# One product for read-out and state update in a chunked RWKV-7 kernel, with a new order of its early turns

## The chip, the cores and the metric

The kernel runs on one core of a Trainium2 chip. Its time is the device time of one execution in microseconds; before the change it is 758.51 us, the median of 3 runs (757.66 to 759.96). The profile shown is of an execution with a span of 757.1 us. Engine names: PE is TensorE, PEld its weight loads, DVE is VectorE, ACT is ScalarE, POOL is GpSimd, SP is SyncE, which here only issues DMAs.

## The reference, cut to what matters

Attention with a recurrent state, then a feed-forward block with a softmax gate and a layer norm:

```python
batch, n_heads, seq, head_dim = (4, 8, 768, 40)
for t in range(S):
    y[:, :, t] = einsum('bhd,bhde->bhe', rt, state)              # read-out, from the state before t
    Sa = einsum('bhde,bhe->bhd', state, at)
    state = state * wt[:, :, None, :] - einsum('bhd,bhe->bhde', Sa, bt) + einsum('bhd,bhe->bhde', vt, kt)

# x: y as 3072 rows of 320
h = x @ w_in                                                     # 320 x 1024
e = exp(h - max(h)); sm = e / (sum(e) + 1e-09)
solu = h * sm
ln = (solu - mean(solu)) / sqrt(var(solu) + 1e-06) * g_ln
out = ln @ w_out                                                 # 1024 x 320
```

The two weight matrices come as 64-bit floats; the kernel brings them in as pairs of 32-bit words and narrows them on the chip.

## The kernel before

The 768 steps are cut into 12 chunks of L = 64 steps. Each chunk has two turns ("slots" below), i = 0 to 23, of 16 heads each; P = 128, Q = 32, D = 40, H = 8, G = 4. Within a chunk the recurrence is solved with the inverse of a triangular matrix. What a slot does is written as generators, and a string gives the order in which their steps are put into the engines' queues. Every engine works through its own queue in that order.

The recurrence of slot i, its read-out, and the crossed term that adds the carried state:

```python
def carried(i, crossed):
    d = st[i]
    for m in range(2):
        for p in range(2):
            for z in range(2):
                c, g = z ^ crossed, 2 * m + z
                nc.tensor.matmul(d["y"][half(p), c, g * L:g * L + L], lhsT=d["sT"][half(z), c, m, half(p)], ...)  # L507

def recurrence(i):
    ...                                                # r1: px (L526), then x = x_own + px on VectorE (L528)
    ...                                                # r2: psT, copied to sT by ScalarE (L539)
    ...                                                # r3: pu (L547), copied to nuT by ScalarE
    y = d["y"] = duo("pyo")
    if ci:
        carried(i, True)
    lamu = d["lamu"] = wide("lamu", 1)
    scores("lamu", nuT, d["rT"], lamu)                 # r4: product on PE, masked by VectorE (L281)
    yield
    t = bank("pnu")
    for g in range(G):
        nc.tensor.transpose(out=t[:, g * P:(g + 1) * P], in_=nuT[:, g, :], identity=ident)
    nc.scalar.copy(out=nu.rearrange("p h c -> p (h c)"), in_=t)                       # r5, L565
    yield
    if ci < NCH - 1:
        t = duo("pst")                                                                # r6
        for j, x in enumerate((vb, nu)):
            for g in range(G):
                for p in range(2):
                    for c in range(2):
                        nc.tensor.matmul(t[half(p), c, g * D:g * D + D], lhsT=kb[half(c), j, 2 * g + p, :],
                                         rhs=x[half(c), G * p + g, 0:D], ...)         # L573
        new = t[:, :, 0:G * D].rearrange("q c (g d) -> q c g d", d=D)
        ...                                            # tot = new + sm on VectorE (L579), sm = tot * factor on GpSimd

def readout(i):
    kb, t = d["kb"], d["y"]
    for j, lam in ((1, d["lamu"]), (0, d["lamv"])):
        for g in range(G):
            for p in range(2):
                h = G * p + g
                for c in range(2):
                    nc.tensor.matmul(t[half(p), c, g * L:g * L + L], lhsT=kb[half(c), j, 2 * g + p, :],
                                     rhs=lam[half(c), h % 2, h // 2, :], ...)         # L593
        if j and i >= 2:
            carried(i, False)
    nc.vector.tensor_tensor(out=of_round[n]["x"]..., in0=t..., in1=d["exT"]..., op=ALU.mult)   # L600
```

The read-out and the state update multiply the same stationary matrices kb, the one with lam (64 columns a head), the other with v and nu (40 columns a head).

The inverse of one chunk takes 32 steps: one that prepares u from the gathered blocks, 30 of two VectorE operations each (L413, L415), and one that sends it off. It serves two slots. bring_inverse fetches it back for a slot, in the layout which that slot's solve needs.

```python
def invert(n):
    ...
    u_dram = of_round[n]["u"] = dram.tile(...)
    for p in range(2):
        nc.sync.dma_start(out=u_dram...[:, :, p], in_=u[half(p)])
    ut = two.tile([P, Q, Q // 2], FP32, tag="ut", name="ut", bufs=1)
    nc.vector.tensor_copy(out=ut, in_=u.rearrange("p c t -> p t c"))                  # L421
    nc.sync.dma_start(out=ut_dram, in_=ut)
    yield

def bring_inverse(i, other=nc.sync):
    ...                                                # 4 DMAs tinv <- ut_dram on `other`, 4 DMAs tinvT <- u_dram on SyncE
```

The narrowing of a weight piece has four steps: two VectorE operations (L162, L164); three ScalarE operations (L167 to L169); one VectorE operation (L171); two GpSimd operations. weights() keeps two pieces under way, so that its steps alternate: one with VectorE's operations of both, and one with ScalarE's operations of the new piece and GpSimd's of the old. After the last piece it forms the column means of the scaled weights (mean, L239) and scales the weights on VectorE (L242).

```python
    pg = bank("pg")
    nc.tensor.transpose(out=pg[:, 0:NF], in_=g_rows, identity=ident[0:NF, 0:NF])
    nc.scalar.copy(out=g_col, in_=pg[:, 0:NF])
    gb = two.tile([P, NF, P], FP32, tag="e", name="gb", bufs=1)
    nc.scalar.mul(out=gb, in_=g_col.unsqueeze(2).to_broadcast([P, NF, P]), mul=1.0 / DFF)
    yield
    mean = bank("mean")
    ...                                                # 8 matmuls into mean
```

The order of a slot (r recurrence, y read-out, I inverse, W weights, a attend of the next slot, s its solve, f and g fronts of later slots, h hidden product of slot i - 6, b and o its end, L a load). The list of numbers says how many steps each I stands for:

```python
EARLY = ("r r a r f r W I r y W r I W W a f a s W a f W a W I f I W s f L W a f", ...)       # i < 6
STEADY = "r b r a r f b b o r o I o r o y o r I o h a f L a s a h f a I h f I s h f h a f h" # i >= 6

def inverse_steps(i):
    if i < 3:
        return [[6, 6, 6, 6], [0, 3, 4, 3], [6, 6, 5, 5]][i]
    return [0, 6, 4, 4] if i % 2 else [6, 6, 3, 3]
...
bring_inverse(0, nc.scalar)                            # in the prologue
...
for i in range(N):
    ...
    if i == 1:
        steps(inv, 8)                                  # the rest of the second inverse
    ...
    if i >= LAG:                                       # LAG = 6
        steps(ws, 99)                                  # what is left of weights()
```

The steps of attend are: kT, vT (each a transposition, copied by ScalarE), psi, rT, lamv, and px0; those of a front end with kx (VectorE, L371), bT and nt. PSUM is used in 2 single banks ("bank"), 2 pairs ("duo") and one pair for h.

Of the kernel before, what the change touches and what calls it, by code (L numbers as in the profile page):

```python
# [52 lines left out]
def kernel(  # L53
# [21 lines left out]

    nc = tc.nc
    B, H, S, D = r.shape
    DM = H * D  # L80
# [57 lines left out]
    ti_t = zeroed(nc.vector, "tinvT", [P, 2, G, L], 2)  # L138
    tn_t = [const.tile([P, H, 2, Q // 2], FP32, name=f"tinv{i}") for i in range(2)]
    sm_t = zeroed(nc.vector, "sm", [P, 2, G, 64], 2)  # L140
    nu_t = [const.tile([P, H, 64], FP32, name=f"nu{i}") for i in range(1)]
# [36 lines left out]
    def weights():  # L178
# [52 lines left out]
        pg = bank("pg")  # L231
        nc.tensor.transpose(out=pg[:, 0:NF], in_=g_rows, identity=ident[0:NF, 0:NF])
        nc.scalar.copy(out=g_col, in_=pg[:, 0:NF])
        gb = two.tile([P, NF, P], FP32, tag="e", name="gb", bufs=1)
        nc.scalar.mul(out=gb, in_=g_col.unsqueeze(2).to_broadcast([P, NF, P]), mul=1.0 / DFF)
        yield
# [45 lines left out]
            out=dst, in0=t[:, :, 0:G * L].rearrange("q p (g c) -> q p g c", g=G),  # L282
            in1=tri.unsqueeze(1).unsqueeze(1).to_broadcast([P, 2, G, L]), op=ALU.mult)

    def wide(name, bufs=1):
        return two.tile([P, 2, G, L], FP32, tag=name, name=name, bufs=bufs)

    st = [dict() for _ in range(N)]
    of_round = [dict() for _ in range(NCH)]
# [107 lines left out]
    def invert(n):  # L397

        nb = of_round[n]["nb"]
        u = two.tile([P, Q // 2, Q], FP32, tag="u", name="u", bufs=1)
        nc.vector.tensor_scalar(out=u[half(0)], in0=nb[half(0)].rearrange("b (c z) t -> b c z t", z=2)[:, :, 0],
                                scalar1=-1.0, scalar2=None, op0=ALU.mult)
        nc.vector.memset(u[half(1)], 0.0)
        for p in range(2):
            nc.vector.memset(u[half(p)].rearrange("b c t -> b (c t)")[:, p:Q * Q // 2:Q + 2], 1.0)
        yield
        for j in range(1, Q - 1):
            m, rows = Q - 1 - j, (j + 1) // 2  # L410
            t = two.tile([P, Q * Q // 8], FP32, tag="prod", name="prod", bufs=1)[:, 0:rows * m] \
                .rearrange("p (c r) -> p c r", c=rows)
            nc.vector.tensor_tensor(out=t, in0=nb[:, j:j + 1, j + 1:Q].to_broadcast([P, rows, m]),  # L413
                                    in1=u[:, 0:rows, j:j + 1].to_broadcast([P, rows, m]), op=ALU.mult)
            nc.vector.tensor_tensor(out=u[:, 0:rows, j + 1:Q], in0=u[:, 0:rows, j + 1:Q], in1=t, op=ALU.subtract)  # L415
            yield
        u_dram = of_round[n]["u"] = dram.tile([64, Q, Q], FP32, tag="u_dram", name="u_dram")
        for p in range(2):
            nc.sync.dma_start(out=u_dram.rearrange("b (c z) t -> b c z t", z=2)[:, :, p], in_=u[half(p)])
        ut = two.tile([P, Q, Q // 2], FP32, tag="ut", name="ut", bufs=1)  # L420
        nc.vector.tensor_copy(out=ut, in_=u.rearrange("p c t -> p t c"))  # L421
        ut_dram = of_round[n]["ut"] = dram.tile([P, Q, Q // 2], FP32, tag="ut_dram", name="ut_dram")
        nc.sync.dma_start(out=ut_dram, in_=ut)
        yield

    def bring_inverse(i, other=nc.sync):

        d = st[i]
        tinvT, tinv = d["tinvT"], d["tinv"] = ti_t[i % 2], tn_t[i % 2]
        n, s = divmod(i, 2)  # L430
        ut, u = of_round[n]["ut"], of_round[n]["u"]
        for q in (0, 2):
            for p in range(2):
                other.dma_start(out=tinv[quarter(q), :, p],
                                  in_=ut[half(p)][homes(q, s)].rearrange("h s t -> s h t"))
        for q in range(4):
            nc.sync.dma_start(out=tinvT[quarter(q), :, :, quarter(q % 2)].rearrange("s p g t -> s (p g) t"),
                              in_=u[homes(q, s)].rearrange("h s t -> s h t"))

    def attend(i):  # L440

        d = st[i]
        kT = transposed("kT", d["kb"][:, 0])
        yield
        vT = transposed("vT", given(i, "v"))
        yield
        psi = d["psi"] = wide("psi")
        scores("psi", kT, d["aT"], psi)
        yield
        rT = d["rT"] = transposed("rT", given(i, "r"), "rT", 2)  # L450
        yield
        lamv = d["lamv"] = wide("lamv", 2)
        scores("lamv", vT, rT, lamv)
        yield
        t = duo("px0")
        for g in range(G):
            for p in range(2):
                for c in range(2):
                    nc.tensor.matmul(t[half(c ^ p), p, g * D:g * D + D], lhsT=psi[half(c), p, g, :],
                                     rhs=given(i, "v")[half(c), G * p + g, 0:D], start=True, stop=True)  # L460
# [38 lines left out]
    def carried(i, crossed):  # L499


        d = st[i]
        for m in range(2):
            for p in range(2):
                for z in range(2):
                    c, g = z ^ crossed, 2 * m + z
                    nc.tensor.matmul(d["y"][half(p), c, g * L:g * L + L], lhsT=d["sT"][half(z), c, m, half(p)],  # L507
                                     rhs=d["rT"][half(z), (G * p + g) // 2, half(c)],
                                     start=crossed and m == 0, stop=False, skip_group_check=True)

    def recurrence(i):
        d = st[i]
        ci, s = divmod(i, 2)
        sm, nu = sm_t[s], nu_t[0]
        kb, vb = d["kb"], given(i, "v")
        x0 = x0_t[i % 2]
        if ci < NCH - 1:
            fac = small.tile([P, 2, G], FP32, tag="fac", name="fac")
# [37 lines left out]
        if ci:  # L556
            d["sT"] = sT
            carried(i, True)
        lamu = d["lamu"] = wide("lamu", 1)
        scores("lamu", nuT, d["rT"], lamu)  # L560
        yield
        t = bank("pnu")
        for g in range(G):
            nc.tensor.transpose(out=t[:, g * P:(g + 1) * P], in_=nuT[:, g, :], identity=ident)
        nc.scalar.copy(out=nu.rearrange("p h c -> p (h c)"), in_=t)  # L565
        yield
        if ci < NCH - 1:
            t = duo("pst")
            for j, x in enumerate((vb, nu)):
                for g in range(G):  # L570
                    for p in range(2):
                        for c in range(2):
                            nc.tensor.matmul(t[half(p), c, g * D:g * D + D], lhsT=kb[half(c), j, 2 * g + p, :],  # L573
                                             rhs=x[half(c), G * p + g, 0:D], start=j == 0 and g == 0, stop=j == 1,
                                             skip_group_check=True)
            new = t[:, :, 0:G * D].rearrange("q c (g d) -> q c g d", d=D)
            if ci:
                tot = two.tile([P, 2, G, D], FP32, tag="tot", name="tot", bufs=1)
                nc.vector.tensor_tensor(out=tot, in0=new, in1=sm[:, :, :, 0:D], op=ALU.add)  # L579
# [4 lines left out]

    def readout(i):
        d, (n, s) = st[i], divmod(i, 2)
        kb, t = d["kb"], d["y"]
        for j, lam in ((1, d["lamu"]), (0, d["lamv"])):
            for g in range(G):
                for p in range(2):  # L590
                    h = G * p + g
                    for c in range(2):
                        nc.tensor.matmul(t[half(p), c, g * L:g * L + L], lhsT=kb[half(c), j, 2 * g + p, :],  # L593
                                         rhs=lam[half(c), h % 2, h // 2, :], start=i < 2 and g == 0 and j == 1,
                                         stop=j == 0, skip_group_check=True)
# [4 lines left out]
        nc.vector.tensor_tensor(out=of_round[n]["x"][:, :, s].rearrange("q g (c t) -> q c g t", c=2),  # L600
                                in0=t[:, :, 0:G * L].rearrange("q c (g t) -> q c g t", g=G),
                                in1=d["exT"].rearrange("q g (c t) -> q c g t", c=2), op=ALU.mult)
        yield

# [87 lines left out]
    def fronts(i):  # L692

        return [j for j in ((4, 5) if i == 0 else (i + AHEAD,)) if j < N]

    EARLY = ("r r a r f r W I r y W r I W W a f a s W a f W a W I f I W s f L W a f",
             "r r a r f g r W I r y W r I W W a f g a s W a f g W a W I f g I W s f g L W a f g")
    STEADY = "r b r a r f b b o r o I o r o y o r I o h a f L a s a h f a I h f I s h f h a f h"
    front_of = {}

    front_of = {}
# [14 lines left out]
    def inverse_steps(i):  # L716

        if i < 3:
            return [[6, 6, 6, 6], [0, 3, 4, 3], [6, 6, 5, 5]][i]
        return [0, 6, 4, 4] if i % 2 else [6, 6, 3, 3]  # L720

    def later(n):
        load(n, "b", "k")
# [2 lines left out]
    with tc.manual_schedule():  # L726
# [12 lines left out]
        turns("f g f g f f g g", {}, f=f, g=g)  # L739
        load(2, "w", "a", "b", "k")  # L740
        turns("a a I a a W", dict(I=99), a=at, I=inv, W=ws)
        bring_inverse(0, nc.scalar)
        turns("a f g a f g f g", {}, f=f, g=g, a=at)
        scatter(1)
        gather(1)
# [5 lines left out]
        for i in range(N):  # L751
            m, more, js = i - LAG, i + 1 < N, fronts(i)
            if i % 2 and (i + 3) // 2 < NCH:
                gather((i + 3) // 2)
            if i == 1:
                steps(inv, 8)
            now = hidden(m) if m >= 0 else None
            parts = dict(r=recurrence(i), y=readout(i), I=inv, W=ws, h=now, b=after, o=before)
            if i >= LAG:
# [51 lines left out]
```

## Time and profile before

| | us |
|---|---|
| time, median of 3 | 758.51 |
| span of the profile | 757.1 |
| PE busy | 630.4 (83%) |
| PEld busy | 451.1 (60%) |
| DVE busy | 455.5 (60%) |
| ACT busy | 270.1 (36%) |
| POOL busy | 118.4 (16%) |
| mean granted TensorE clock | 0.886 of full |
| pst (L573), busy, 1408 records | 30.6 |
| read-out (L593), busy, 1536 records | 32.5 |

Busy time is a sum over instructions; a matmul's end is modelled, so its mean time is longer than its share of a packed stream. A 32-bit float matmul leaves two records. A wait is given with the engine or DMA whose event came last before it ended. The share of the whole span mixes an early stage (slots 0 to 5, in which the weights are narrowed too) with the later slots, in which the feed-forward products run beside the recurrence; each has to be read by itself.

### The profile page before, as it was taken

The page shows a single profiled execution, that of the slowest core. Times are in us where ns is not written, and L with a number is a line of the kernel's source. Part 1 is how long each engine was busy: PE and PEld are TensorE (multiplying, and loading weights), DVE is VectorE, ACT ScalarE, POOL GpSimd, SP SyncE. Part 2 cuts the span into 40 slices and gives each one's busy share as a digit, 9 for nine tenths or more (in the row PEclk, how much of TensorE's full clock was granted, in tenths as well). Part 3 has the DMA queues.
Part 4 walks back from the last instruction along what each step waited for, and adds up shares of the span by engine and source line. Part 5 has one row for each costly group of instructions (what it writes and reads, how often), then busy time and mean ns, then how long its engine had stood idle before and what let it go on. Part 6 is the DMA issues. An engine that isn't in the chain of part 4 may idle for free.

```text
span 757.1 us, 28253 instructions
## 1 busy us (share of the span) xinstructions
PE 630.4 (83%) x12281; PEld 451.1 (60%) x12281; DVE 455.5 (60%) x1258; ACT 270.1 (36%) x631; POOL 118.4 (16%) x204
## 2 busy tenths in 40 slices
PE   6335758566584899999999999999999899998997
PEld 4334646455473666666676767767667566654554
DVE  3654764746645485768758677687585772334442
ACT  4113325333353142434333533444343332332222
POOL 4102132321232011111111011101110000000000
PEclk9656575795775799999999999999999999999999
DMA  8946455355354434544553635545414322101001
GB/s 138 162 73 119 88 109 103 66 104 118 68 114 94 65 63 93 93 94 77 110 101 57 127 72 94 101 85 98 92 35 82 69 48 38 27 15 26 11 8 35
DMA packets 269804, 60.01 MB, mean 79 GB/s; under 512 B 255465, under 2 KB 265329, under 8 KB 269681
## 3 DMA queue, kind: packets, MB, share of 16 engines
q1 hardware_dynamic: 264592, 52.66, 38.3%
q10 hardware_dynamic: 5088, 5.55, 2.9%
q8 instruction: 97, 1.59, 0.9%
q14 instruction: 27, 0.21, 0.1%
HBM read 40.08 MB, written 13.37 MB: 71 GB/s over the span
## 4 chain that ended last, share of the span: by engine, by line
PE 65%; DVE 17%; DMA 6%; ACT 5%; issue 4%; SPq 2%; ACTq 0%; POOL 0%; DVEq 0%
PE po L666 14%; PE h L621 14%; DVE prod L413 5%; DVE u L415 5%; PE plnT L661 3%; PE pyo L593 3%; PE pcx L340 3%; PE plamv L279 2%; PE pst L573 2%; PE pcum L327 2%; DMA blk<-blk_dram 2%; PE py L481 2%; DMA blk_dram<-nt 2%; PE pyo L507 2%; PE px L526 1%
## 5 line engine op out<-in xcount | busy, mean ns | idle before, releaser
L621 PE MATMUL h<-w_in,xT 128*128 128x512 f32 (+1 forms) x288 | 126.8, 627 | 3.9 <-DVE e L638 3.9
L666 PE MATMUL po<-w,lnT 128*128 128x320 f32 x384 | 118.8, 442 | 0.0
L415 DVE TENSOR_TENSOR u<-u,prod 128x30 f32<-128x30 f32 (+4 forms) x360 | 98.3, 273 | 12.4
L413 DVE TENSOR_TENSOR prod<-blk,u 128x30 f32<-128x30 f32 (+4 forms) x360 | 99.1, 275 | 10.3
L666 PEld LDWEIGHTS po<-w,lnT 128*128 128x128 f32 x384 | 67.6, 190 | 23.6 <-issue 2.9
L330 POOL TENSOR_TENSOR kx<-raw_b,inv 128x320 f32<-128x320 f32 x24 | 20.9, 873 | 255.2 <-ACT inv L328 204.6
L621 PEld LDWEIGHTS h<-w_in,xT 128*128 128x128 f32 (+1 forms) x288 | 37.8, 189 | 30.6 <-issue 28.7
L631 DVE TENSOR_REDUCE nmax<-h 128x1 f32<-128x1024 f32 x24 | 29.4, 1223 | 40.7 <-PE h L621 40.7
L671 ACT ACTIVATE osb<-po,rs 128x320 f32<-128x320 f32 x24 | 12.6, 527 | 106.0 <-PE po L666 94.6
L481 PE MATMUL py<-tinv,nt 32*32 32x32 f32 x768 | 21.1, 207 | 29.7 <-DMA tinv<-ut_dram 17.8
L281 DVE TENSOR_TENSOR lamv<-plamv,cst 128x512 f32<-128x512 f32 x24 | 16.6, 690 | 43.0 <-PE plamv L279 43.0
L340 PE MATMUL pcx<-cst,lw 128*128 128x132 f32 x192 | 35.2, 318 | 8.2 <-ACT vT L262 8.1
L600 DVE TENSOR_TENSOR x<-pyo,kx 128x512 f32<-128x512 f32 x24 | 16.6, 691 | 42.0 <-PE pyo L593 41.0
L340 PEld LDWEIGHTS pcx<-cst,lw 128*128 128x128 f32 x192 | 30.7, 220 | 17.3 <-ACT vT L262 8.3
L635 ACT ACTIVATE e<-h,nmax 128x1024 f32<-128x1024 f32 x24 | 26.7, 1114 | 37.3 <-DVE nmax L631 37.3
L662 ACT COPY lnT<-plnT 128x512 f32<-128x512 f32 x48 | 27.6, 586 | 33.9 <-PE plnT L661 33.8
L638 DVE TENSOR_TENSOR e<-h,e 128x1024 f32<-128x1024 f32 x24 | 29.4, 1224 | 14.6 <-ACT e L635 14.0
L653 POOL TENSOR_TENSOR rs<-c,mhalf 128x1 f32<-128x1 f32 x24 | 13.2, 548 | 157.0 <-DVE c L652 157.0
L481 PEld LDWEIGHTS py<-tinv,nt 32*32 32x32 f32 x768 | 17.8, 118 | 32.0 <-issue 18.5
L496 ACT ACTIVATE tinvT<-pz 32x256 f32<-32x256 f32 x48 | 17.9, 373 | 51.3 <-PE pz L481 51.0
L661 PE MATMUL plnT<-cst,e 128*128 128x128 f32 x192 | 30.6, 290 | 5.7 <-DVE e L638 5.4
L580 POOL TENSOR_TENSOR sm<-tot,fac 128x320 f32<-128x320 f32 x20 | 14.7, 737 | 118.6 <-DVE tot L579 98.7
(107 smaller groups left out, 1160.9 us busy)
## 6 DMA issues: line engine op xcount, KB each, us to landing
blk<-blk_dram SPq DMA_DIRECT2D x24, 256.0 KB
raw_w<-in_w_dram SPq DMA_DIRECT2D x24, 160.0 KB
raw_a<-in_a_dram SPq DMA_DIRECT2D x24, 160.0 KB
raw_b<-in_b_dram SPq DMA_DIRECT2D x24, 160.0 KB
raw_k<-in_k_dram SPq DMA_DIRECT2D x24, 160.0 KB
v<-in_v_dram SPq DMA_DIRECT2D x24, 160.0 KB
r<-in_r_dram SPq DMA_DIRECT2D x24, 160.0 KB
out_dram<-osb SPq DMA_DIRECT2D x24, 160.0 KB
```

Of the source, the lines that this page charges most:

```text
L340: nc.tensor.matmul(t[:, g * 132:g * 132 + 132], lhsT=pair(lw, 2 * j + g), rhs=cst[:, lo:lo + 132], start=True, stop=True)
L413: nc.vector.tensor_tensor(out=t, in0=nb[:, j:j + 1, j + 1:Q].to_broadcast([P, rows, m]), in1=u[:, 0:rows, j:j + 1].to_broadcast([P, rows, ...
L415: nc.vector.tensor_tensor(out=u[:, 0:rows, j + 1:Q], in0=u[:, 0:rows, j + 1:Q], in1=t, op=ALU.subtract)
L481: nc.tensor.matmul(t[quarter(out), c:c + Q], lhsT=lhs(p, g), rhs=rhs(p, g), start=True, stop=True)
L593: nc.tensor.matmul(t[half(p), c, g * L:g * L + L], lhsT=kb[half(c), j, 2 * g + p, :], rhs=lam[half(c), h % 2, h // 2, :], start=i < 2 and ...
L621: nc.tensor.matmul(h[:, j * 512:j * 512 + 512], lhsT=of_round[i // 2]["xT"][rows, kt, i % 2 * P:i % 2 * P + P], rhs=w_in[rows, 4 if kt == ...
L631: nc.vector.tensor_reduce(out=nmax, in_=h, axis=AX.X, op=ALU.max, negate=True)
L635: nc.scalar.activation(out=e, in_=h, func=AF.Exp, bias=nmax, accum_out=esum)
L638: nc.vector.tensor_tensor(out=q, in0=h, in1=e, op=ALU.mult)
L661: nc.tensor.transpose(out=t[:, j * P:(j + 1) * P], in_=q[:, f * P:(f + 1) * P], identity=ident)
L662: nc.scalar.copy(out=lnT[:, fs.start:fs.stop].rearrange("p f t -> p (f t)"), in_=t)
L666: nc.tensor.matmul(o[:, 0:DM], lhsT=lnT[:, f, :], rhs=w2[:, f, :], start=f == 0, stop=f == NF - 1)
```

## The change

The 40 columns of v and of nu are put behind the 64 columns of lamv and lamu of each head, in one tile of 104 columns. v is copied there by GpSimd, nu by ScalarE straight from PSUM. The read-out then yields both: 64 columns of y and 40 columns of the new state, 104 a head, 416 of the 512 of a PSUM bank. The separate state product pst goes away. In the last chunk only the 64 columns are computed.

Beside it, the order of the queues changes. A slot of the early stage has ten steps of weights() instead of nine, so that ScalarE's part of a piece stands at other places than VectorE's. The second inverse is done within slot 0 (8 steps at each I), and the 8 steps at the head of slot 1 go. In the steady order one of the four I goes and its steps are spread over the other three. ut is copied and sent before the second half of u. SyncE issues all DMAs of the first bring_inverse, not ScalarE. weights() has one step more, between g_col and gb.

```diff
-    def wide(name, bufs=1):
-        return two.tile([P, 2, G, L], FP32, tag=name, name=name, bufs=bufs)
+    def wide(name, width, bufs=1):
+        return two.tile([P, 2, G, width], FP32, tag=name, name=name, bufs=bufs)
@@ invert
-        for p in range(2):
-            nc.sync.dma_start(out=u_dram.rearrange("b (c z) t -> b c z t", z=2)[:, :, p], in_=u[half(p)])
         ut = two.tile([P, Q, Q // 2], FP32, tag="ut", name="ut", bufs=1)
         nc.vector.tensor_copy(out=ut, in_=u.rearrange("p c t -> p t c"))
         ut_dram = of_round[n]["ut"] = dram.tile([P, Q, Q // 2], FP32, tag="ut_dram", name="ut_dram")
-        nc.sync.dma_start(out=ut_dram, in_=ut)
+        for p in range(2):
+            nc.sync.dma_start(out=u_dram.rearrange("b (c z) t -> b c z t", z=2)[:, :, p], in_=u[half(p)])
+            if p == 0:
+                nc.sync.dma_start(out=ut_dram, in_=ut)
@@ weights
         nc.scalar.copy(out=g_col, in_=pg[:, 0:NF])
+        yield
         gb = two.tile([P, NF, P], FP32, tag="e", name="gb", bufs=1)
@@ attend
+        lamv = d["lamv"] = wide("lamv", L + D, 2)
+        nc.gpsimd.tensor_copy(out=lamv[:, :, :, L:], in_=given(i, "v").rearrange("q (m z) d -> q z m d", z=2)[:, :, :, 0:D])
...
-        lamv = d["lamv"] = wide("lamv", 2)
-        scores("lamv", vT, rT, lamv)
+        scores("lamv", vT, rT, lamv[:, :, :, 0:L])
@@ recurrence
-        lamu = d["lamu"] = wide("lamu", 1)
-        scores("lamu", nuT, d["rT"], lamu)
+        lamu = d["lamu"] = wide("lamu", L + D)
+        scores("lamu", nuT, d["rT"], lamu[:, :, :, 0:L])
...
-        nc.scalar.copy(out=nu.rearrange("p h c -> p (h c)"), in_=t)
+        nc.scalar.copy(out=lamu[:, :, :, L:], in_=t.rearrange("q (m z c) -> q z m c", m=G, z=2)[:, :, :, 0:D])
...
-            t = duo("pst")
-            for j, x in enumerate((vb, nu)):
-                ...                                    # the 32 matmuls of L573
-            new = t[:, :, 0:G * D].rearrange("q c (g d) -> q c g d", d=D)
+            new = y[:, :, 0:G * (L + D)].rearrange("q c (g w) -> q c g w", g=G)[:, :, :, L:]
@@ readout
-        kb, t = d["kb"], d["y"]
+        kb, t, W = d["kb"], d["y"], L + D
+        used = W if n < NCH - 1 else L
...
-                        nc.tensor.matmul(t[half(p), c, g * L:g * L + L], lhsT=kb[half(c), j, 2 * g + p, :],
-                                         rhs=lam[half(c), h % 2, h // 2, :], ...)
+                        nc.tensor.matmul(t[half(p), c, g * W:g * W + used], lhsT=kb[half(c), j, 2 * g + p, :],
+                                         rhs=lam[half(c), h % 2, h // 2, 0:used], ...)
@@ order
-    EARLY = ("r r a r f r W I r y W r I W W a f a s W a f W a W I f I W s f L W a f", ...)
-    STEADY = "r b r a r f b b o r o I o r o y o r I o h a f L a s a h f a I h f I s h f h a f h"
+    EARLY = ("r r a r W f r W W I r y W r W I a f a W s a f a W I W f s W I f a W L f", ...)
+    STEADY = "r b r a r f b b o r o I o r o y o r I o h a f L a s a h f a I h f s h f h a f h"
...
-            return [[6, 6, 6, 6], [0, 3, 4, 3], [6, 6, 5, 5]][i]
-        return [0, 6, 4, 4] if i % 2 else [6, 6, 3, 3]
+            return [[8, 8, 8, 8], [0, 3, 4, 3], [6, 6, 5, 5]][i]
+        if i < LAG:
+            return [0, 5, 5, 4] if i % 2 else [5, 5, 4, 4]
+        return [0, 7, 7] if i % 2 else [6, 7, 5]
...
-        bring_inverse(0, nc.scalar)
+        bring_inverse(0)
...
-            if i == 1:
-                steps(inv, 8)
```

The columns of carried and of the product on VectorE after the read-out move from steps of 64 to steps of 104 in the same way.

More of the change, by code (lines that the diff above doesn't have):

```diff
@@ L140 @@
     sm_t = zeroed(nc.vector, "sm", [P, 2, G, 64], 2)
-    nu_t = [const.tile([P, H, 64], FP32, name=f"nu{i}") for i in range(1)]
     y_mid = const.tile([P, 2, G, Q], FP32, name="y_mid")
@@ L422, in invert, with bring_inverse @@
         ut_dram = of_round[n]["ut"] = dram.tile([P, Q, Q // 2], FP32, tag="ut_dram", name="ut_dram")
-        nc.sync.dma_start(out=ut_dram, in_=ut)
+        for p in range(2):
+            nc.sync.dma_start(out=u_dram.rearrange("b (c z) t -> b c z t", z=2)[:, :, p], in_=u[half(p)])
+            if p == 0:
+                nc.sync.dma_start(out=ut_dram, in_=ut)
         yield
-    def bring_inverse(i, other=nc.sync):
+    def bring_inverse(i):
         d = st[i]
@@ L433, in bring_inverse @@
             for p in range(2):
-                other.dma_start(out=tinv[quarter(q), :, p],
+                nc.sync.dma_start(out=tinv[quarter(q), :, p],
                                   in_=ut[half(p)][homes(q, s)].rearrange("h s t -> s h t"))
@@ L446, in attend @@
         yield
-        psi = d["psi"] = wide("psi")
+        psi = d["psi"] = wide("psi", L)
         scores("psi", kT, d["aT"], psi)
@@ L502, in carried @@
         d = st[i]
+        W = L + D
         for m in range(2):
@@ L506, in carried @@
                     c, g = z ^ crossed, 2 * m + z
-                    nc.tensor.matmul(d["y"][half(p), c, g * L:g * L + L], lhsT=d["sT"][half(z), c, m, half(p)],
+                    nc.tensor.matmul(d["y"][half(p), c, g * W:g * W + L], lhsT=d["sT"][half(z), c, m, half(p)],
                                      rhs=d["rT"][half(z), (G * p + g) // 2, half(c)],
@@ L513, in recurrence @@
         ci, s = divmod(i, 2)
-        sm, nu = sm_t[s], nu_t[0]
-        kb, vb = d["kb"], given(i, "v")
+        sm = sm_t[s]
         x0 = x0_t[i % 2]
@@ L564, in recurrence @@
             nc.tensor.transpose(out=t[:, g * P:(g + 1) * P], in_=nuT[:, g, :], identity=ident)
-        nc.scalar.copy(out=nu.rearrange("p h c -> p (h c)"), in_=t)
+        nc.scalar.copy(out=lamu[:, :, :, L:], in_=t.rearrange("q (m z c) -> q z m c", m=G, z=2)[:, :, :, 0:D])
         yield
         if ci < NCH - 1:
-            t = duo("pst")
-            for j, x in enumerate((vb, nu)):
[L570 to L575, printed above, removed]
-            new = t[:, :, 0:G * D].rearrange("q c (g d) -> q c g d", d=D)
+            new = y[:, :, 0:G * (L + D)].rearrange("q c (g w) -> q c g w", g=G)[:, :, :, L:]
             if ci:
@@ L592, in readout @@
                     for c in range(2):
-                        nc.tensor.matmul(t[half(p), c, g * L:g * L + L], lhsT=kb[half(c), j, 2 * g + p, :],
-                                         rhs=lam[half(c), h % 2, h // 2, :], start=i < 2 and g == 0 and j == 1,
+                        nc.tensor.matmul(t[half(p), c, g * W:g * W + used], lhsT=kb[half(c), j, 2 * g + p, :],
+                                         rhs=lam[half(c), h % 2, h // 2, 0:used], start=i < 2 and g == 0 and j == 1,
                                          stop=j == 0, skip_group_check=True)
@@ L600, in readout @@
         nc.vector.tensor_tensor(out=of_round[n]["x"][:, :, s].rearrange("q g (c t) -> q c g t", c=2),
-                                in0=t[:, :, 0:G * L].rearrange("q c (g t) -> q c g t", g=G),
+                                in0=t[:, :, 0:G * W].rearrange("q c (g w) -> q c g w", g=G)[:, :, :, 0:L],
                                 in1=d["exT"].rearrange("q g (c t) -> q c g t", c=2), op=ALU.mult)
@@ L694, in fronts @@
         return [j for j in ((4, 5) if i == 0 else (i + AHEAD,)) if j < N]
-    EARLY = ("r r a r f r W I r y W r I W W a f a s W a f W a W I f I W s f L W a f",
-             "r r a r f g r W I r y W r I W W a f g a s W a f g W a W I f g I W s f g L W a f g")
-    STEADY = "r b r a r f b b o r o I o r o y o r I o h a f L a s a h f a I h f I s h f h a f h"
+    EARLY = ("r r a r W f r W W I r y W r W I a f a W s a f a W I W f s W I f a W L f",
+             "r r a r W f g r W W I r y W r W I a f g a W s a f g a W I W f g s W I f g a W L f g")
+    STEADY = "r b r a r f b b o r o I o r o y o r I o h a f L a s a h f a I h f s h f h a f h"
+    front_of = {}
     front_of = {}
```

## The prediction

> **What bounds the kernel now.** I read four views in this order: the page's slices, busy time by stage, PE's waits in the early stage, and the timeline of one steady slot. A "slot" is one turn of the loop over i; its start is taken as the first pu matmul (L547).
>
> ```profile
> PE   6335758566584899999999999999999899998997
> DVE  3654764746645485768758677687585772334442
> PEclk9656575795775799999999999999999999999999
> ```
> Each digit is a fortieth of the span (18.9 us). Up to slice 14 no engine is full and TensorE's granted clock is low; from there PE is at 9. So there are two regimes. Busy time by stage, slots 0 to 5 on a line each, then slots 6 to 21, then the last two with the tail (columns: stretch, length, busy us of PE, PEld, DVE, ACT, POOL, granted clock, DMA share, GB/s):
>
> ```profile
> 57.90:95.30 37.40, 23.46 (x469) 19.22 (x468) 23.10 (x74) 13.08 (x33) 8.72 (x12) 0.64 0.55 103
> 95.30:127.40 32.10, 20.74 (x457) 17.42 (x456) 18.42 (x56) 12.84 (x33) 9.86 (x14) 0.66 0.57 117
> 127.40:157.90 30.50, 19.36 (x491) 15.98 (x490) 21.98 (x66) 11.34 (x31) 8.25 (x13) 0.73 0.31 60
> 157.90:190.00 32.10, 19.63 (x490) 16.27 (x490) 14.26 (x50) 11.30 (x33) 8.41 (x15) 0.70 0.60 120
> 190.00:218.40 28.40, 19.77 (x490) 16.64 (x489) 18.89 (x58) 10.98 (x30) 7.25 (x13) 0.68 0.38 77
> 218.40:257.60 39.20, 24.96 (x504) 18.87 (x503) 17.52 (x56) 12.44 (x33) 8.26 (x15) 0.72 0.51 95
> 257.60:655.50 397.90, 383.74 (x8368) 271.37 (x8368) 275.43 (x742) 156.04 (x355) 50.56 (x85) 0.99 0.42 79
> 655.50:757.10 101.60, 90.67 (x657) 53.19 (x656) 37.34 (x69) 27.90 (x53) 4.38 (x8) 0.97 0.08 21
> ```
> Slots 0 to 5 take 199.7 us with DVE and PE each busy some 57 to 64%: waits rule there. From 257.6 to 655.5 PE is busy 96% at clock 0.99: PE's own work is the time. PE's waits between 45.6 and 257.6 us:
>
> ```profile
> PE py L481 <- DMA tinv<-ut_dram: 17.8, 3, 8.1
> PE py L481 <- ACT vT L262: 11.6, 2, 6.1
> PE pcx L340 <- ACT vT L262: 8.1, 1, 8.1
> PE pyo L593 <- DVE lamu L281: 4.7, 6, 3.6
> PE mean L239 <- ACT tinvT L496: 3.3, 1, 3.3
> ```
> (total us, times, longest.) ScalarE's vT is late because the narrowing's L167 stands ahead of it and waits for VectorE's L162, which stands behind six steps of the inverse: ScalarE idles 8.09, 9.45 and 8.92 us before L167 in slots 0, 2 and 4. The DMA waits fall in slots 1, 3 and 5. In a steady slot:
>
> ```profile
> 409.61 0.69 PE L593 MATMUL pyo<-lamu,kx 64*64 64x64 f32 x32
> 410.12 0.41 PE L507 MATMUL pyo<-rT,sT 64*64 64x64 f32 x16
> 410.36 0.65 PE L593 MATMUL pyo<-lamv,kx 64*64 64x64 f32 x32
> 410.93 1.34 PE L666 MATMUL po<-w,lnT 128*128 128x320 f32 x4
> 412.21 0.68 PE L573 MATMUL pst<-v,kx 64*64 64x40 f32 x32
> 412.69 0.66 PE L573 MATMUL pst<-nu,kx 64*64 64x40 f32 x32
> 413.28 1.34 PE L666 MATMUL po<-w,lnT 128*128 128x320 f32 x4
> ```
> From start to start, the read-out's 80 records take 1.32 us and the state update's 64 take 1.07: 16.5 and 16.7 ns each, although one streams 64 columns and the other 40. That is a floor per record, not streaming. (One fp32 matmul leaves two records: 16 calls per operand, 32 records.)
>
> **What the Trainium skill says.** "FP8 and Floating Point Precision", TensorE Precision Notes: true FP32 takes 4 passes. The trace agrees: eight po matmuls of 320 columns take 4.31 us, 1.68 ns a column, which is 4 cycles at the 2.4 GHz of "TensorE: Matmul & The Clock Gate". That page, Back-to-back issue gap, has a floor of about 25 ns for matmuls up to 64 columns; the floor is here too, but at 16.5 ns a record, and the trace decides. Its section Architectural detail calls ScalarE and VectorE strict FIFOs: the 8 to 9 us stalls ahead of L167 agree. "TensorEngine Tiling (Array Packing)", Key Properties, lets tiles run independently: four 64x64 tiles at 64 columns would need 64x4/2.4/4 = 26.7 ns a matmul, and 33 ns are measured, so all four must overlap.
>
> **Part 1, 104 columns.** Removed: 64 records of pst a slot, 1.07 us, in 22 slots. Added: 40 columns to each of the 32 read-out matmuls. At four passes, 2.4 GHz (clock 0.99 here) and four tiles, a matmul streams 104x4/2.4/4 = 43.3 ns, 21.7 a record, over the floor. Read-out: 64 x 21.7 = 1.39 us, before 64 x 16.5 = 1.06. Net -1.07 + 0.33 = -0.74 us; were the 3.2 ns by which 16.5 exceeds 13.3 an overhead that adds, -0.53. I take -0.74. In the 16 steady slots 6 to 21 PE is the bound, so all of it counts: **-11.8 us**. The sum tot no longer waits for pst (15 waits, 24.2 us of DVE), but DVE isn't the bound there. POOL gains one copy of 320 elements (0.46 us by L360), ACT's nu copy shrinks from 512 to 320 elements (0.585 to 0.43), neither on the path. The read-out now needs nu: ScalarE ends it at 409.27, the read-out begins at 409.61, so it fits.
>
> **Part 2, the steady order.** In odd slots four inverse steps after kx keep nmax waiting until 401.05, with h done at 399.7; PE then idles 0.76 us for x (L528) and 0.33 for sT. Now seven steps lie ahead of kx and none behind: from 395.87, 7 x 0.61 us end at 400.1, kx at 400.75, nmax 0.36 us earlier. pnt (400.12) must wait some 0.6 us for kx, but inside the same gap. -0.36 in each of 8 pairs: **-2.9**.
>
> **Part 3, the prologue.** ScalarE no longer issues four DMAs (48.33 to 50.98) ahead of x0 and bT, for which PE idled 3.12 us. SyncE issues ut earlier by one DMA but then tinv and tinvT in turn. I take **-2**.
>
> **Part 4, the early slots.** I laid VectorE's queue out anew: 0.58 us an inverse step (two operations), 1.5 the first, 0.9 to 1.0 a narrowing step, 0.6 each psi, lamv, kx, nt, x and lamu. Ten W a slot, an even number, means that each slot begins with a VectorE step; ScalarE's follows after inverse steps no longer stand between.
> - Slot 0 gets 8 more steps (4.7 us) and the ut copy, loses the 8.06 us wait: DVE runs from lamu at 60.3 to nt at 89, before 95.1. Slot 1 begins at 89.4 instead of 95.3 (2 us of it the prologue's).
> - Slot 1 loses 8 steps ahead of lamu (3.55 us of PE) and the wait for ut. Its own first inverse step waits for blk, some 10 us after nt, at 99.5; from there 10 steps and five products end about 112. Slot 2 begins at 113.5, before 127.4: another 8.
> - Slot 2 is filled by VectorE, 26.5 us instead of 30.5: -4.
> - Slot 3 keeps its chain: nt, scatter, blk_dram, gather, blk took 15.6 us (157.4 to 172.98), tinv queues behind it. No gain.
> - Slot 4 loses the 5.5 us wait for vT: 23.5 instead of 28.4, -5.
> - Slot 5 keeps the blk chain, but mean (6.79 us), gb (ScalarE waited 4.84 before it) and the eight scalings (3.29 on the chain) move into that wait. -10, less 3 because mean holds one of two PSUM banks until its last scaling: -7.
>
> Slots 0 to 5 and prologue: 6 + 8 + 4 + 0 + 5 + 7 = **-30 us**. The tail after 655.5 is untouched.
>
> Sum: 758.5 - 11.8 - 2.9 - 30 = 713.8. Waits that I can't see in a queue laid out by hand will cost some; I add 4: **718 us**.
>
> **Rivals.** (a) The product is no cheaper: if 104 columns ran with only two tiles overlapped, a record costs 43 ns, the read-out 2.77 us and each slot gains 0.6 us of work: the steady part +10 us, the total near 740. Against it, the 33 ns a matmul at 64 columns. (b) The early gain is a change of wait: blk and tinv come through one SyncE queue, and the read-out now needs nu, behind a narrowing step of ScalarE (1.3 us). If slots 0, 2 and 4 end sooner only to wait longer for blk, half of the 30 goes: near 733. For it, the 6.95 and 5.09 us that VectorE waited for blk in slots 3 and 5; against it, that chain starts from nt, which itself comes earlier. (c) VectorE becomes the steady bound through seven steps ahead of kx: pnt's wait isn't hidden, +0.6 in nine odd slots, near 724. (d) All is hidden and the clock, higher where PE idles less, adds to it: near 705.
>
> **Range and chances.** The steady part is between -18 and -5, the early part between -40 and -15. Both at their weak ends make 738, at their strong ends 700; eight times in ten 704 to 733. Faster by over 2% is below 743.3: only rival (a) with a poor early part gets there. 0.94 faster, 0.04 same, 0.02 slower.
>
> **What would show it.** Steady read-out of 64 records near 1.4 us, pst gone, pairs of slots 47.6 us instead of 49.4. ScalarE's waits before L167 gone from slots 0, 2, 4; PE's wait of vT with them; the three waits of py for tinv down to two; mean inside slot 5's wait and L242 no longer on the chain. Slot 6 beginning near 228 instead of 257.6. Wrong: a read-out over 2 us, pnt waiting for kx with the pair not shorter, or slots 1, 3, 5 longer by what 0, 2, 4 lose.

## The result and the profile after

The changed kernel takes 731.85 us (median of 4 runs, 729.76 to 734.0) against 758.78 us before; the ratio is 0.9645, 95% interval 0.9613 to 0.9677. That is 27 us less, inside the predicted range, but only two thirds of the 40 us predicted. The profile shown is of an execution with a span of 728.0 us.

PE's slices of the span on the page of the changed kernel (each digit a fortieth, 18.2 us):

```profile
PE   6436636665766899999999999999999899979997
```

The two regimes are still there. Slot 6 begins at 244.7 us instead of 257.6; the prediction had it near 228. Busy time of slots 0 to 5, one on a line (columns as in the prediction: stretch, length, busy us of PE, PEld, DVE, ACT, POOL, clock, DMA share, GB/s). A slot is counted from its first pu matmul to that of the next.

```profile
56.60:92.40 35.80, 22.15 (x405) 17.93 (x404) 28.98 (x86) 14.51 (x37) 11.07 (x15) 0.71 0.50 95
92.40:126.50 34.10, 17.21 (x392) 14.34 (x392) 17.35 (x47) 12.81 (x34) 10.66 (x15) 0.70 0.63 125
126.50:153.10 26.60, 19.02 (x424) 15.62 (x424) 22.67 (x67) 11.80 (x33) 9.30 (x16) 0.68 0.36 73
153.10:184.80 31.70, 17.80 (x424) 14.91 (x424) 16.75 (x54) 11.65 (x34) 8.69 (x16) 0.73 0.61 122
184.80:208.50 23.70, 17.19 (x426) 14.21 (x426) 20.13 (x59) 11.45 (x33) 8.79 (x16) 0.78 0.41 77
208.50:244.70 36.20, 24.62 (x439) 19.18 (x439) 16.54 (x50) 9.01 (x23) 5.32 (x10) 0.72 0.53 99
```

In slots 2 and 4 VectorE is now busy 85% of the slot, which is what the change was after. In slots 1, 3 and 5 no engine is busy more than some 68%, and slot 1 is longer than it was. Set beside the prediction:

| part | before us | after us | difference | predicted |
|---|---|---|---|---|
| prologue, to the first pu | 57.88 | 56.64 | -1.2 | -2 |
| slot 0 | 37.46 | 35.78 | -1.7 | -4 |
| slot 1 | 32.05 | 34.05 | +2.0 | -8 |
| slot 2 | 30.47 | 26.61 | -3.9 | -4 |
| slot 3 | 32.09 | 31.70 | -0.4 | 0 |
| slot 4 | 28.42 | 23.67 | -4.8 | -5 |
| slot 5 | 39.27 | 36.27 | -3.0 | -7 |
| slots 6 to 21 | 387.7 | 370.6 | -17.1 | -14.7 |
| slot 22 to the end | 111.8 | 112.7 | +0.9 | 0 |

The last 4 us of the prediction's sum were an allowance. A selection of PE's waits between 45.7 and 244.7 us (total us, times, longest):

```profile
PE py L484 <- DMA tinv<-ut_dram: 34.2, 10, 12.8
PE pz L484 <- DVE kx L372: 12.1, 2, 7.1
PE mean L240 <- ACT gb L236: 3.9, 1, 3.9
PE pyo L589 <- ACT lamu L568: 3.3, 6, 0.7
PE pcx L341 <- ACT vT L263: 1.0, 2, 0.7
```

The waits put down to vT, 19.7 us before, are down to 1.0. The wait for tinv has grown from 17.8 us to 34.2, with one piece of 12.8 in slot 1. And one steady slot:

```profile
318.47 0.94 PE L589 MATMUL pyo<-lamu,kx 64*64 64x104 f32 x32
319.24 0.41 PE L511 MATMUL pyo<-rT,sT 64*64 64x64 f32 x16
319.47 0.90 PE L589 MATMUL pyo<-lamv,kx 64*64 64x104 f32 x32
320.29 2.42 PE L662 MATMUL po<-w,lnT 128*128 128x320 f32 x8
```

From start to start the read-out takes 0.77 + 0.82 = 1.59 us without the carried term: 24.8 ns a record, not the 21.7 predicted. And the eight po records now stand together: in the trace they run from 320.29 to the next operation at 322.64, 2.35 us. Before, the same eight and pst between them took from 410.93 to 414.55, 3.62 us. So pst took 1.27 us out of the slot, not 1.07.

### The profile page after: what moved, and what is told of

The parts are those of the page before. It is cut to its first block, busy times and chain, and to the rows that moved or that the text cites. A ratio compares the mean times of both kernels' runs of the same rounds, so it can differ in the third digit from the quotient of the medians.

```text
span 728.0 us, 25509 instructions
## 1 busy us (share of the span) xinstructions
PE 605.3 (83%) x10873; PEld 431.6 (59%) x10873; DVE 467.5 (64%) x1258; ACT 267.2 (37%) x631; POOL 128.5 (18%) x228
## 4 chain that ended last, share of the span: by engine, by line
PE 58%; DVE 22%; DMA 7%; issue 5%; ACT 4%; SPq 3%; POOL 1%; ACTq 0%; DVEq 0%; POOLq 0%
PE po L662 14%; PE h L617 12%; DVE prod L414 7%; DVE u L416 6%; PE pyo L589 4%; PE plnT L657 3%; PE pcx L341 2%; PE pcum L328 2%; DVE nmax L627 2%; PE plamv L280 2%; PE py L484 2%; DMA raw_b<-in_b_dram 2%; PE pyo L511 2%; PE pvT L261 2%; PE ppsi L280 1%
## 5 line engine op out<-in xcount | busy, mean ns | idle before, releaser
L662 PE MATMUL po<-w,lnT 128*128 128x320 f32 x384 | 114.8, 438 | 0.0
L414 DVE TENSOR_TENSOR prod<-blk,u 128x30 f32<-128x30 f32 (+4 forms) x360 | 107.0, 297 | 11.8 <-DMA blk<-blk_dram 1.0
L416 DVE TENSOR_TENSOR u<-u,prod 128x30 f32<-128x30 f32 (+4 forms) x360 | 101.5, 282 | 12.4
L484 PE MATMUL py<-tinv,nt 32*32 32x32 f32 x768 | 20.6, 202 | 34.2 <-DMA tinv<-ut_dram 34.2
L634 DVE TENSOR_TENSOR e<-h,e 128x1024 f32<-128x1024 f32 x24 | 29.4, 1225 | 14.6 <-ACT e L631 14.2
L341 PEld LDWEIGHTS pcx<-cst,lw 128*128 128x128 f32 x192 | 29.1, 209 | 14.9 <-ACT y_mid L496 8.5
L341 PE MATMUL pcx<-cst,lw 128*128 128x132 f32 x192 | 33.6, 307 | 5.3 <-ACT y_mid L496 3.4
L657 PE MATMUL plnT<-cst,e 128*128 128x128 f32 x192 | 29.9, 285 | 5.7 <-DVE e L634 5.4
```

What stands on the lines that cost most here:

```text
L341: nc.tensor.matmul(t[:, g * 132:g * 132 + 132], lhsT=pair(lw, 2 * j + g), rhs=cst[:, lo:lo + 132], start=True, stop=True)
L484: nc.tensor.matmul(t[quarter(out), c:c + Q], lhsT=lhs(p, g), rhs=rhs(p, g), start=True, stop=True)
L634: nc.vector.tensor_tensor(out=q, in0=h, in1=e, op=ALU.mult)
L657: nc.tensor.transpose(out=t[:, j * P:(j + 1) * P], in_=q[:, f * P:(f + 1) * P], identity=ident)
L662: nc.tensor.matmul(o[:, 0:DM], lhsT=lnT[:, f, :], rhs=w2[:, f, :], start=f == 0, stop=f == NF - 1)
```

## What held slot 1

The chain that ended last between 85 and 130 us in the changed kernel, from the load of b on (start, length, what). Pieces of issue under 0.2 us are left out; three dots stand for longer cuts:

```profile
94.63 5.42 DMA raw_b<-in_b_dram
...
101.03 0.73 POOL parts L174
101.83 0.73 POOL w_in L175
102.59 0.80 DVE parts L162
...
106.06 0.23 ACT parts L167
106.32 2.94 DMA bits<-in_moe_w_in_dram
109.32 0.31 SPq L436
...
110.66 2.07 DMA tinv<-ut_dram
112.87 1.03 PE py L484 x30
```

And SyncE's queue over the same time:

```profile
92.43 0.55 SPq L423 DMA_DIRECT2D u_dram<-u  x1
93.07 2.38 SPq L306 DMA_DIRECT2D raw_b<-in_b_dram  x2
95.55 3.62 SPq L306 DMA_DIRECT2D raw_k<-in_k_dram  x2
99.26 2.74 SPq L389 DMA_DIRECT2D blk_dram<-nt  x4
103.49 1.12 SPq L396 DMA_DIRECT2D blk<-blk_dram  x2
109.32 1.79 SPq L436 DMA_DIRECT2D tinv<-ut_dram  x4
```

SyncE's queue in the kernel before, in slot 0 and then around the start of slot 3:

```profile
76.73 3.47 SPq L305 DMA_DIRECT2D raw_b<-in_b_dram  x2
83.21 1.31 SPq L305 DMA_DIRECT2D raw_k<-in_k_dram  x2
...
157.75 1.41 SPq L305 DMA_DIRECT2D raw_b<-in_b_dram  x2
159.25 1.78 SPq L305 DMA_DIRECT2D raw_k<-in_k_dram  x2
161.12 4.69 SPq L388 DMA_DIRECT2D blk_dram<-nt  x4
```

Read together: the second inverse now ends at the end of slot 0, and its u_dram stands in SyncE's queue ahead of the load of b and k (L306). Before, those loads were issued at 76.73, well within slot 0. Now they go out at 93.07, and the scatter (blk_dram<-nt) behind them at 99.26, although nt was ready at 93.0. The kernel before had the same order in slots 3 and 5 all along: in slot 3 nt was ready at 157.4, and the scatter went out at 161.12, behind the loads. The change gave slot 1 the order of slot 3. GpSimd's queue stands still for raw_b (11.87 us) with the narrowing's L175 behind it; VectorE's L162 waits 6.97 us for L175, since the second W ahead of the read-out put it there; ScalarE follows; and the tinv issue, by the profile, waits for the landing of a weight piece. So the change took a wait of VectorE out and put one through four queues in.

## The experiments

Times are medians of 4 runs unless marked; each ratio is to the kernel before on the same chip.

**c: L forward in slot 0.** Only the string of slot 0 is edited:

```diff
- "... W I a f g a W s a f g a W I W f g s W I f g a W L f g"
+ "... W I a f g a W s L a f g a W I W f g s W I f g a W f g"
```

> Theory: slot 1 of the changed kernel (34.05 us) is long because the load of b and k for the next chunk (step L) stands behind u_dram in SyncE's queue, which waits for the end of the second inverse. It lands late, GpSimd stands still for raw_b (11.9 us), with it the narrowing, VectorE (7.0 us), ScalarE, and the tinv DMAs. With L ahead of the third I in slot 0, slot 1 takes 22 to 27 us and the kernel 720 to 724 instead of 731.85. Rival 1: tinv waits for the blocks (nt, scatter, gather) ahead of it in SyncE's queue, whatever L does: slot 1 stays over 32 and the kernel within 729 to 734.

Measured: 725.97 us, ratio 0.9562 (0.9531 to 0.9593). Slot 1 takes 28.72 us. SyncE's queue:

```profile
79.05 1.98 SPq L306 DMA_DIRECT2D raw_b<-in_b_dram  x2
81.13 2.99 SPq L306 DMA_DIRECT2D raw_k<-in_k_dram  x2
...
93.31 2.83 SPq L389 DMA_DIRECT2D blk_dram<-nt  x4
99.84 1.13 SPq L396 DMA_DIRECT2D blk<-blk_dram  x2
101.07 5.00 SPq L436 DMA_DIRECT2D tinv<-ut_dram  x4
```

The loads go out 14 us sooner, the scatter at 93.31. Slot 1 loses 5.3 us: the place of L was about half of what kept the gain of slot 1 away, and rival 1 falls as the whole account. But slot 1 stays longer than the 22 to 27 us of the theory, and the kernel stays above its 720 to 724. Part of what is left is in the last three lines: tinv stands behind a gather (blk<-blk_dram) that waits 3.6 us for the scatter to land, as rival 1 has it, and its four issues then take 5 us.

**d: L forward in slots 2 and 4 too** (the same move in the other early string).

> L moved forward in slots 0, 2 and 4. Theory: in slots 3 and 5 too, scatter and gather stand behind the four issues of L (3.4 to 4.5 us) and the narrowing behind raw_b, so each loses another 3 to 4 us: 712 to 718. Rival: there the chain is set by nt and the trips through DRAM alone: the same as L moved in slot 0 alone, within 2 us.

Measured: 717.25 us, ratio 0.9449 (0.9414 to 0.9484). Slot 3 goes from 31.99 us in c to 28.62, slot 5 from 35.06 to 30.05. The rival falls; the same queue order cost slots 3 and 5 time. The kernel before had it there too; what L forward would gain in that kernel wasn't tried. In slot 5 PE's 3.9 us wait for gb is gone: it was raw_b again, by way of GpSimd's part of the last narrowing.

**e: the scalings right behind mean in slot 5.** A string of its own for slot 5:

```diff
- "r r a r W f r W W I r y W r W I a f a W s a f a W I W f s W I f a W L f"
+ "r r a r W f r W W I r y W r W W W W W I a f a s a f a I f s I f a L f"
```

> As d, and in slot 5 the four scaling steps stand right behind mean, so that its PSUM bank comes free before vT. Theory: mean's bank costs PE 4.95 us before pz and 2.2 us in three short waits of slot 5: another 4 to 7 us less than d, 706 to 713. Rival: pz waits for kx because kx stands behind five inverse steps in VectorE's queue; only the two scalings ahead of it count, 1 to 2 us less than d.

Measured: 712.66 us, ratio 0.939 (0.9355 to 0.9425); slot 5 takes 25.36 us. PE's longest wait in slot 5 of d, and then pz and kx in slot 5 of e:

```profile
PE pz L484 <- DVE kx L372: 5.4, 1, 5.4
```

```profile
219.62 0.69 PE L484 MATMUL pz<-tinvT,y_mid 32*32 32x32 f32 x32
222.95 0.68 DVE L372 TENSOR_TENSOR kx<-paT,kx 128x512 f32<-128x512 f32 x1
```

pz doesn't read kx. It waited for a bank: mean held one and paT, which kx empties, the other. With mean's bank free, pz no longer waits: it now runs 3.3 us ahead of kx, which still stands behind five inverse steps. So the rival falls. Slot 5 loses 4.7 us, at the low end of the theory's 4 to 7: of the three short waits, 2.3 us in d, 1.5 us stay. Run once more:

> The version with L forward in the even early slots and the scalings behind mean once more, beside the next two: 710 to 716.

Measured: 713.24 us, ratio 0.9399 (0.9358 to 0.9441).

**f: the second inverse back in two parts.**

```diff
-            return [[8, 8, 8, 8], [0, 3, 4, 3], [6, 6, 5, 5]][i]
+            return [[6, 6, 6, 6], [0, 3, 4, 3], [6, 6, 5, 5]][i]
...
+            if i == 1:
+                steps(inv, 8)
```

> The changed kernel with the second inverse as before (6 steps at each I of slot 0, 8 at the head of slot 1). What the prediction held: the move is worth some 8 us, so 738 to 741. Theory now: moved into slot 0 the inverse delays raw_b and gains nothing; put back, slot 0 is 4 to 5 us shorter and slot 1 some 32 long: 723 to 730.

Measured: 728.17 us, ratio 0.9565 (0.9511 to 0.9619). Slots 0 and 1 together take 67.1 us, against 69.8 in the changed kernel and 64.7 in c. So this part of the change, as it was made, gained nothing; the intervals of the whole times just touch. In f PE waits for lamu again, in slot 1:

```profile
PE py L484 <- DMA tinv<-ut_dram: 4.9, 2, 4.0
PE pyo L589 <- DVE parts L164: 4.5, 1, 4.5
```

The profile names a narrowing step of VectorE, which ends at the same time (100.38) as ScalarE's copy of nu into lamu (100.33). Both halves of lamu are late behind the eight steps: VectorE's product comes after them, and ScalarE's copy stands behind a narrowing step that waits 3.8 us for VectorE.

**k: the same taken back from e**, where L stands forward.

> The same with the second inverse back in two parts (6 steps at each I of slot 0, 8 at the head of slot 1). Theory: once raw_b no longer waits behind it, the inverse within slot 0 is worth what VectorE's eight steps ahead of lamu cost PE in slot 1 less the 8 steps that slot 0 grows by: 2 to 3 us, so 714 to 717. Rival (the size predicted): 8 us or more, over 720.

Measured: 714.55 us, ratio 0.9403 (0.9359 to 0.9447). Slots 0 and 1 take 66.8 us in its trace, against 64.0 and 64.6 in the two of e. So the traces give the move 2 to 3 us once raw_b is out of its way; the whole times of k and e overlap and can't separate that. The size predicted falls.

**a: the product alone**, with every order as before.

> The kernel before with the product of 104 columns alone, all orders as before. Theory: per steady slot the read-out grows by 0.50 us (25 ns a record) and pst goes with 1.07 us and about 0.2 us that po lost around it: -0.77 in 16 slots, -12 us, the early slots unchanged within 2 us: 745 to 748. Rival: pst cost its 1.07 us only, -0.57 a slot: 749 to 751.

Measured: 747.63 us, ratio 0.9851 (0.9812 to 0.989), -12.3 us. A steady pair of slots takes 47.90 us instead of 49.43: -0.765 a slot. The theory holds, and pst cost what it took out of po too. Slots 0 to 5 sum to 198.95 us, before 199.76.

**i: the old steady order** (four I; 6 6 3 3 and 0 6 4 4) in the changed kernel.

> The changed kernel with the old steady order (four I, steps 6 6 3 3 and 0 6 4 4 from slot 6 on). Theory: the new order is worth the shorter wait before pu, 0.2 to 0.4 us a pair of slots, in 8 pairs: 733 to 736. Rival: the order is worth all that the product does not explain by its streaming, 0.77 a pair: 737 to 739.

Measured: 733.43 us, ratio 0.9673 (0.9627 to 0.9719). Whole times alone don't settle it, but the trace does: a pair takes 47.91 us, in the changed kernel 47.53. The order is worth 0.38 us a pair. The rival falls by this reading.

**h: the old early strings** in the changed kernel.

> The changed kernel with the old strings of the early stage (nine W a slot), the second inverse still within slot 0 and the steady order new. Theory: the ten W are worth the waits of vT in slots 2 and 4 (3.9 and 4.8 us) and the mean in slot 5 (3 to 5 us): 742 to 746. Rival: the stalls only change place: 731 to 735.

Measured: 744.17 us, ratio 0.9803 (0.9763 to 0.9843). The wait for vT is back:

```profile
PE py L484 <- ACT vT L263: 16.1, 2, 9.1
PE pcx L341 <- ACT vT L263: 12.2, 1, 12.2
```

The new strings are worth some 12 us, as much as the product; they were the part of the early change that worked. The theory has the total right, but only part of where it comes from. Slots 2, 4 and 5 take 3.3, 3.2 and 2.8 us more than in the changed kernel, slots 1 and 3 take 1.6 and 1.1 less, and slot 0 takes 5.9 more: there, with eight inverse steps at each I in the old string, PE waits 12.2 us for vT, where the kernel before waited 8.1. Whether the ten W or the new places of the other steps do it, h doesn't separate.

**g: 120 columns** (16 columns of zeros more a head; one timed run).

```diff
-        lamv = d["lamv"] = wide("lamv", L + D, 2)
+        lamv = d["lamv"] = wide("lamv", L + 56, 2)
```

and so for lamu, the copies behind them and the steps of y.

> The product widened to 120 columns (16 columns of zeros more a head). If a record costs what four overlapped tiles need to stream it plus a fixed 3 ns, a half of the read-out takes 0.89 us (28 ns a record) where 104 columns took 0.79. If only the floor and streaming counted, 0.80 (25 ns). If tiles overlapped less with width, over 1.0.

Measured: 736.01 us; the read-out of one slot:

```profile
321.89 1.05 PE L589 MATMUL pyo<-lamu,kx 64*64 64x120 f32 x32
322.76 0.41 PE L511 MATMUL pyo<-rT,sT 64*64 64x64 f32 x16
323.00 1.00 PE L589 MATMUL pyo<-lamv,kx 64*64 64x120 f32 x32
```

The first half takes 0.87 us, the second 0.93 in all steady slots: 28.1 ns a record. With 17.0 ns at 64 columns (1.09 us before, the slot's two halves) and 24.8 at 104, the step is 0.20 ns a column, which is the streaming of four overlapped tiles, with some 3 to 4 ns on top of it (the prediction's estimate for 104 columns alone was 21.7). At 40 columns pst had 16.7 ns, so there the floor holds.

**j: tinv ahead of gather** in slots 1, 3 and 5, on top of e.

```diff
+            early = i < LAG and i % 2 == 1
+            if early:
+                bring_inverse(i + 1, second=False)     # the four tinv DMAs alone
             if i % 2 and (i + 3) // 2 < NCH:
                 gather((i + 3) // 2)
...
-                bring_inverse(i + 1)
+                bring_inverse(i + 1, first=not early)
```

> As e, but in slots 1, 3 and 5 the four tinv DMAs are issued ahead of gather. Theory: py waits 23.4 us in all for tinv, most of it in slots 1 and 3, where gather, waiting for the landing of the scatter, stands ahead of tinv in SyncE's queue; out of that queue tinv lands 3 to 6 us sooner and each of the two slots loses 2 to 4 us: 705 to 709. Rival: the same slots are held by the blocks (VectorE's first inverse step waits for them), which the four issues delay by 2 us: 711 to 716.

Measured: 710.34 us, ratio 0.9367 (0.9329 to 0.9406), the fastest version here, though between the theory's 705 to 709 and the rival's 711 to 716. The whole times of j and e overlap. Slot 1 of j, and two of PE's waits in slot 3 of j:

```profile
93.00:118.90 25.90, 18.14 (x390) 15.13 (x390) 17.18 (x47) 12.45 (x33) 10.75 (x15) 0.74 0.66 136
```

```profile
PE pz L484 <- DMA tinvT<-u_dram: 3.2, 1, 3.2
PE py L484 <- DMA tinv<-ut_dram: 0.6, 1, 0.6
```

Slot 1 goes from 28.64 us in both traces of e to 25.9: the theory holds there. Slot 3 took 29.90 and 30.58 in e and takes 31.1 in j: there the theory fails. tinv does come sooner, and PE's wait for it falls from 6.9 and 7.2 us in e to 0.6. But PE then waits 3.2 us for tinvT, which still stands behind gather in SyncE's queue, and the clock granted in the slot is lower (0.62, against 0.67 in both traces of e). The rival isn't shown either: VectorE waits 6.2 us before its first inverse step, against 4.5 and 4.7 in e, but by the profile PE doesn't wait for that.

## Why the prediction was right and wrong, point by point

- **The bounds.** The two regimes, PE's work from slot 6 on and waits before it, were read rightly; each part of the sum belonged to the regime it was put in.
- **Part 1, 104 columns.** -11.8 us predicted, -12.3 measured in a, but by two errors that cancel. The read-out grew by 0.50 us, not 0.33: the 3.2 ns above streaming, which the prediction named as a possible overhead, do add. And pst took 1.27 us out of the slot, not 1.07, because the po records on its two sides ran 0.2 us longer than without it. That the sum came out is luck. Four tiles overlap at 104 columns (24.8 ns a record, where two would need 43) and at 120, so rival (a) falls.
- **Part 2, the steady order.** -0.36 us a pair predicted, 0.38 in i. pnt waits 0.56 us in the changed kernel, inside the gap, as predicted; rival (c) falls. Slots 6 to 21 came out 2.4 us better than the sum of both parts, which is 1.84 us a pair. Slots 6 and 7 are 2.67 us shorter; with the old early strings (h) slot 6 takes 21.35 us and not 19.91, so part of this belongs to the early order. Slots 20 and 21 are 2.90 us shorter, but they take 43.3 us in this trace and 44.9 in those of c and e, so that part may not be the change's.
- **Part 3, the prologue.** -1.2 against -2. A single pair of traces can't settle it: the eleven traces with the new prologue reach the first pu after 54.96 to 57.43 us, the two with the old one (before and a) after 57.88 and 58.75. The means, 56.4 and 58.3, differ by 1.9, which agrees with the prediction.
- **Part 4, slots 2, 3 and 4.** -3.9, -0.4 and -4.8 against -4, 0 and -5. In slots 2 and 4, where VectorE's queue set the time, laying it out anew gave the right numbers. Slot 3's 0 took over a chain of 15.6 us from nt to blk as it stood; 3.7 us of it were the scatter behind L, which the prediction didn't see, and d, with L forward, took 3.4 us out of the slot.
- **Slot 0** failed in size: -1.7 against -4. VectorE's 30 paired inverse steps took 18.84 us together, 0.63 each, where 0.58 was put in. That is 1.5 of the 2.3 us missing; the rest isn't traced.
- **Slot 1** is the step that failed. "Slot 1 loses 8 steps ahead of lamu (3.55 us of PE) and the wait for ut" was right about lamu: the read-out now waits 0.65 us for nu instead. Wrong was "its own first inverse step waits for blk, some 10 us after nt": that step came 14.2 us after nt (107.12 against 92.96), and what held PE was tinv, with one wait of 12.8 us. The prediction laid VectorE's queue out anew and left SyncE's as it was. L, u_dram and the scatter had changed places in time, and with raw_b went GpSimd's queue, the narrowing, and VectorE's place for it. c shows that the place of L cost 5.3 us of the 10 missing, j that tinv behind gather costs another 2.7. The last 2 us, 25.95 in j against some 24 predicted, no run explains.
- **Slot 5** failed by 4 us: the allowance of 3 us for mean's bank was too small (e: 4.7), and mean was late by 3.9 us, again through raw_b.
- **Rival (b)** held in part: of the early gain of 30 us, 11.7 came from slots 0 to 5 and 1.2 from the prologue. Its total, near 733, is the nearest of all to what was measured. It named the queue, SyncE's, but the loss isn't spread as it said: slots 2 and 4 keep their gain and slot 3 doesn't grow, while slots 1 and 5 lack 10 and 4 us. And the tile that comes late in slot 1 is tinv, held through the order of SyncE's and GpSimd's queues, more than blk. That order stood in the queue of the kernel before, in slots 3 and 5, but not in its list of waits.

Open: by the profile the tinv issue in slot 1 waits for the landing of a weight piece on ScalarE's queue (4.7 us in the changed kernel, 3.1 in c). Whether that transfer holds it, or something that ends at the same time, wasn't tried. Why slot 3 took 28.6 us in d and 29.9 to 31.1 in the later versions is open too. The new order of ut and u and the added step of weights() weren't tried by themselves.

## What to carry to other kernels

When work moves from one place in a program to another, follow the transfers it issues as well: in a DMA queue that is worked in order, a store that waits for the moved work holds every load and store behind it, and the cost appears on an engine that has nothing to do with it. Lay out the queues of all engines after the change, not only that of the engine that was busy, and look whether another stage of the old profile already has the order that the change makes. A wait for an operation whose result isn't read is a wait for its buffer; ask what else holds one.

## What the runs showed of the hardware that I had not expected

- Small fp32 matmuls in 64x64 tiles cost 16.7 ns a record at 40 columns, 17.0 at 64, 24.8 at 104 and 28.1 at 120. Two products that share their stationary matrices are cheaper as one even when the columns only add up: 1.59 us for 104 columns against 1.09 and 1.07 for 64 and 40.
- A short block of 64x64 matmuls between 128x128 ones lengthens its neighbours: eight po records took 2.35 us together, and 2.55 with pst between them. In the steady slots of the kernel before, four po records take 1.08 us between 128x128 products, 1.17 ahead of a 64x64 one and 1.27 between two of these: about 0.1 us at each change. The Trainium skill, "TensorEngine Tiling (Array Packing)", Key Properties, says that a change of tiling mode drains TensorE; these times agree with that, though no run here separates it from other causes.
